# Operand sums of the second half moved one slot forward, score products moved two slots back, in a fused attention and gated-FFN kernel

## The chip, the cores and the metric

The kernel runs on one core of a Trainium2 chip. The metric is the time of one execution on the device in microseconds (us). The kernel before takes 808.18 us, the median of three runs (807.96 to 809.92). The execution that was profiled took 805.96 us and its span from the first to the last instruction is 804.2 us.

## The reference, cut to what matters

```python
# q, k, v: (4, 6016, 256); w_gate, w_val: (256, 1536); w_out: (1536, 256)
qn = q / (norm(q, axis=1) + 1e-6);  kn = k / (norm(k, axis=1) + 1e-6)   # norm over the 6016 tokens
s  = kn.T @ qn / tau                       # (4, 256, 256), contracted over tokens
a  = softmax(s)                            # over the last axis
x  = (v @ a).reshape(24064, 256)
out = (sigmoid(x @ w_gate) * (x @ w_val)) @ w_out      # (24064, 256)
```

So there are four batches. Each needs a 256x256 score matrix and two vectors of norms before its tokens can pass through the gated FFN.

## The kernel before, in words

**Folding.** The kernel never forms `x`. It multiplies the softmax weights of a batch into `w_gate` and `w_val` once (the tiles `gh_G` and `gh_H`) and feeds the transposed `v` straight into these.

**Tiles and slots.** A batch has 47 tiles of 128 tokens, in 12 chunks of four tiles (512 tokens), the last of three. A chunk has 12 *slots*, one for each 128 of the 1536 hidden columns. The loop at the end of the kernel runs over batches `b`, chunks `ci` and slots `f`; the order of instructions on every engine is the order in which this loop writes them (a manual schedule), and the engines run against each other only through semaphores.

**A slot.** `glu` (L660) issues two matmuls into `ps_gate`, a tanh of it on the scalar engine (ACT) into `g_sb` (L680), two matmuls into `ps_val`, and one operation on the vector engine (DVE), which writes 128 rows of the hidden tile `hT` (L683). `ps_gate` and `ps_val` have two buffers each. Between the two pairs of matmuls, `run_work` issues a share of the output product of the *previous* chunk, one part in (12 - f) of what is left.

**The output product.** `out_work` (L720) multiplies `hT` of the previous chunk by `w_out` with seven products in place of eight per 2x2 block, which is Winograd's form of Strassen's scheme. Its operands are sums of blocks of `hT`, five kinds, m = 0 to 4, made by `a_sum` (L694) on DVE into the tile `sums` (L705). A chunk's sums are made in two halves: g = 0 from hidden rows 0 to 5 of the chunk's slots, g = 1 from rows 6 to 11. The first half is made in slots 7 to 11 of the chunk itself (`OWN_SLOTS`), the second while the next chunk runs (`NEXT_SLOTS`), since its `hT` is complete only then. In the order of `ORDER`, each product runs i = 0 to 5; from i = 3 on it reads the second half. For a chunk of four tiles that is 84 products, seven in a slot. The product `z1` (sum m = 1) of the first pair of tiles reaches i = 3 as the first product of slot 3, `x2` (m = 3) in slot 5, `y2` (m = 2) in slot 6, `z2` (m = 0) in slot 7 and `v2` (m = 4) in slot 8. For a chunk of three tiles `z1` reaches i = 3 in slot 2. `sums` of g = 1 has one buffer.

**The next batch's scores.** While batch b is in its FFN, `side_work` (L931) places the work for batch n = b + 1 in the slots, after `glu` and the operand sums of the slot. For b = 1 and 2 the token tiles come in six groups of eight (the last of seven), a group for every 16 slots from s0 on. `score_sums` (L340) makes operand sums of q and k, again five kinds, into the tiles `qs`: m = 0 in slot s0, 2 in s0 + 3, 3 in s0 + 6, 4 in s0 + 9 on DVE (L351, L359, L364), and m = 1 by two DMA transfers. `queue_scores` (L922) puts the group's 28 matmuls into a queue, and `run_scores` (L925) takes an even share of them in each slot, from s0 + 3 to s0 + 18. The products that read m = 4 begin with number 12 of the 28, which comes in slot s0 + 11. After the last group come folds of the squares (`acc_fold`, L312, line L315, DVE) in slots 95, 96, 98 and 100 of the batch, and `score_out` copies the scores away in slots 103 and 105.

Of the kernel before, what the change touches and what calls it, by code (L numbers as in the profile page):

```python
# [45 lines left out]
    (0, "x2"), (0, "y2"), (0, "z2"), (0, "v2"),  # L46
    (1, "x2"), (1, "y2"), (1, "z2"), (1, "v2"),
)
NEXT_SLOTS = {1: 1, 3: 3, 4: 2, 5: 0, 6: 4}
OWN_SLOTS = {7: 1, 8: 3, 9: 2, 10: 0, 11: 4}  # L50


# [1 line left out]
def kernel(  # L54
# [109 lines left out]
    t0, nt = groups0[0]  # L164
# [529 lines left out]
    def a_sum(b, ci, g, m):  # L694

        nt = groups[ci][1]
        half = nt // 2
        hT = hts[b, ci]
        if (b, ci, g) not in sums:
            sums[b, ci, g] = spool.tile(  # L700
                [P, len(A_SUMS), FC // 4, CH // 2], BF16, tag=f"s{g}", name="sums", bufs=2 - g
            )
        (r0, k0), op, (r1, k1) = A_SUMS[m]
        f0, f1 = g * (FC // 2), (g + 1) * (FC // 2)
        nc.vector.tensor_tensor(  # L705
            out=sums[b, ci, g][:, m, :, : half * P],
            in0=hT[:, f0 + k0 : f1 : 2, ds(r0 * half * P, half * P)],
            in1=hT[:, f0 + k1 : f1 : 2, ds(r1 * half * P, half * P)],
            op=op,
        )  # L710
# [94 lines left out]
    def run_work(work, share):  # L805

        upto = sum(w[0] for w in work) * share
        done = 0
        while work and done < upto:
            cost, fn, *args = work.pop(0)  # L810
            fn(*args)
            done += cost

    def store():
        while stores:
            b, ci = stores.pop(0)
            t0, nt = groups[ci]
            nc.sync.dma_start(out=out_rows[b][:, t0 : t0 + nt, :], in_=ffn.pop((b, ci))[:, :nt, :])
# [112 lines left out]
    def side_work(b):  # L931


        side = {}

        def at(slot, fn, *a):
            side.setdefault(divmod(slot, FC), []).append((fn, a))

        for ci in range(NCH):
            nb, nci = (b, ci + 1) if ci + 1 < NCH else (b + 1, 0)  # L940
            lb, lci = (b, ci + 2) if ci + 2 < NCH else (b + 1, ci + 2 - NCH)
            if nb < B:
                at(ci * FC + 2, transpose_v, nb, nci)
            if lb < B:
                at(ci * FC + (10 if (b, ci) == (0, 0) else 0), load_v, lb, lci)
            if (b, ci) == (0, 0):
                for i in range(FC // TPC):
                    at(8, copy_w_out, i)
                for n, m in enumerate((1, 0, 3, 2, 4)):
                    for i in range(FC // TPC):  # L950
                        at(11 + 2 * n, sum_w_out, m, i)
        n = b + 1
        if n == B:
            return side
        first, last = (14 if b == 0 else 0), 8 * FC
        wide = [(t, min(2 * TPC, NT - t)) for t in range(0, NT, 2 * TPC)]
        at(first, acc_start, n)
        for g, (t0, nt) in enumerate(groups if b == 0 else []):
            s0 = first + g * (last - first) // NCH
            at(max(FC - 3, s0 - 12), load_qk, n, t0, nt)  # L960
            for u in range(nt):
                at(first + (t0 + u) * (last - first) // NT, score, n, t0, u)
            for w in range(2):
                at(s0 + 1 + 4 * w, narrow_square, n, g, w)
                slot = s0 + 3 + 4 * w
                at(slot + 2 if w == 0 and slot % FC == 8 else slot, narrow_add, n, g, w)
        step = (last - first) / len(wide)
        for g, (t0, nt) in enumerate(wide if b else []):
            s0 = first + int(g * step)
            halves = [(0, nt - TPC), (TPC, TPC)]  # L970
            if s0 >= 24:
                at(s0 - 24, load_qk, n, t0, nt)
            for i in range(4):
                at(s0 + 3 * i, acc_square, n, t0, 1 - i // 2, halves, i % 2)
            for w in range(2):
                at(s0 + 11 - 6 * w, acc_add, n, t0, w, halves)
            for m in (0, 2, 3, 4):
                at(s0 + 3 * max(0, m - 1), score_sums, n, t0, m, halves)
            ahead = 0 if g == 0 else 5
            at(s0 + 1 - ahead, score_sums, n, t0, 1, halves)  # L980
            at(s0 + 6 - ahead, score_sum_q, n, t0, halves)
            end = first + int((g + 1) * step) + 3
            at(s0 + 3, queue_scores, n, t0, halves)
            for slot in range(s0 + 3, end):
                at(slot, run_scores, s0 + 3, end, slot)
        if n + 1 < B:
            for g, (t0, nt) in enumerate(wide[:2]):
                at(NCH * FC - 24 + 16 * g, load_qk, n + 1, t0, nt)
        s0 = 8 * FC + 2
        if b == 0:  # L990
            at(s0, acc_fold, n, 0, (2, 1))
            at(s0 + 1, acc_fold, n, 1, (2, 1))
            at(s0 + 3, norms_mm, n)
            at(s0 + 4, root_seed, n)
            at(s0 + 4, root_steps, n)
            at(s0 + 10, norms_inv, n)
            at(s0 + 11, spread_both, n)
            at(s0 + 13, read_row, n)
        else:
            at(s0 - 3, acc_fold, n, 1, (4,))  # L1000
            at(s0 - 2, acc_fold, n, 1, (2, 1))
            at(s0, acc_fold, n, 0, (4,))
            at(s0 + 2, acc_fold, n, 0, (2, 1))
            at(s0 + 5, score_out, n, 0)
            at(s0 + 6, norms_mm, n)
            at(s0 + 7, score_out, n, 1)
            at(s0 + 7, root_seed, n)
            at(s0 + 7, root_steps, n)
            at(s0 + 12, norms_inv, n)
            at(s0 + 12, spread_both, n)  # L1010
            at(s0 + 14, read_row, n)
            at(s0 + 14, score_blocks, n)
        at(s0 + 22, scale_x, n, 0)
        at(s0 + 24, scale_x, n, 1)
        at(s0 + 25, exps, n, 0)
        at(s0 + 26, exps, n, 1)
        at(s0 + 28, all_sums, n)
        at(s0 + 28, gh_tiles, n)
        for i, piece in enumerate(gh_order):
            slot = s0 + 29 + 2 * i  # L1020
            if slot < NCH * FC:
                at(slot, gh, n, piece, *((pss, "s"), (psm, "m"))[i % 2])
            else:
                spill.setdefault((n, *divmod(slot - NCH * FC, FC)), []).append((gh, (n, piece, psm, "m")))
        return side
# [7 lines left out]
    def gh_pieces(ns):  # L1033
        for n in ns:
            gh(0, gh_first[n], *gh_banks[n % 4])

    prev = None
    for b in range(B):
        side = side_work(b)
        for ci in range(NCH):  # L1040
            final = (b, ci) == (B - 1, NCH - 1)
            for f in range(FC):
                mid = gh_mid.get(f) if (b, ci) == (0, 0) else None
                if prev is not None:
                    mid = lambda: run_work(work, 1 / max(1, FC - final - f))
                elif mid is not None:
                    mid = lambda ns=mid: gh_pieces(ns)
                glu(b, ci, f, mid)
                if prev is not None:
                    if f == 4:  # L1050
                        store()
                    if f + final in NEXT_SLOTS and prev != (0, 0):
                        a_sum(*prev, 1, NEXT_SLOTS[f + final])
                if f in OWN_SLOTS and not final and (b, ci) != (0, 0):
                    a_sum(b, ci, 0, OWN_SLOTS[f])
                for fn, a in spill.get((b, ci, f), []) + side.get((ci, f), []):
                    fn(*a)
                if (b, ci) == (0, 0):
                    gh_pieces(gh_end.get(f, ()))
            prev = (b, ci)  # L1060
            if not final:
                work = out_work(*prev)
# [39 lines left out]
```

## Time and profile before

The page gives each engine's busy time over the span of 804.2 us.

| Engine | busy us | share | instructions |
|---|---|---|---|
| TensorE, matmul (PE) | 781.5 | 97% | 6861 |
| TensorE, weight load (PEld) | 497.0 | 62% | 6875 |
| VectorE (DVE) | 705.0 | 88% | 1228 |
| ScalarE (ACT) | 513.8 | 64% | 891 |
| GpSimd (POOL) | 396.8 | 49% | 618 |

The groups that the change touches, or that stand next to it on their engine:

| Line | work | count | mean ns |
|---|---|---|---|
| L683 | `hT` from `g_sb` and `ps_val`, DVE | 576 | 672 |
| L705 | `sums`, DVE | 460 | 582 |
| L364 | `qs`, m = 3 and 4, DVE | 28 | 682 (median) |
| L129 | matmul into `ps_gate` or `ps_val` | 1152 each | 375 |
| L129 | matmul into `ps_o` that reads `sums` | 2670 | 219 |

The duration of a matmul is its latency. Matmuls overlap, so 375 ns isn't the time that one adds to the stream. In the same way one DVE operation begins some 0.07 us before the record of the one in front of it ends. For both, the distance from start to start is what counts. In every view, "A <- B" means that A waited and B is what it waited for.

### The profile page before, as it was taken

To read this page: it belongs to the slowest core of one execution; us is meant where nothing else is said; L and a number is where in the kernel's file an instruction comes from. 1 tells how busy PE (TensorE), PEld (TensorE's weight loads), DVE (VectorE), ACT (ScalarE), POOL (GpSimd) and SP (SyncE) were. 2 spreads that over 40 slices of the span, in tenths; PEclk is the share of its full clock that TensorE was granted. 3 is DMA by queue.
4 is the path that set the end of the run, shared out by engine and by line. 5 is a ranking of instruction groups with operands and counts; after the bars stand their busy time and mean duration, and the time that the engine had idled before them with its cause. 6 is when DMAs were issued, how large, how long until landed. Compare 5 with 4: busy or idle time off the path is not lost.

```text
span 804.2 us, 18203 instructions
## 1 busy us (share of the span) xinstructions
PE 781.5 (97%) x6861; PEld 497.0 (62%) x6875; DVE 705.0 (88%) x1228; ACT 513.8 (64%) x891; POOL 396.8 (49%) x618
## 2 busy tenths in 40 slices
PE   3899999999999999999999999999999999999998
PEld 2556666666666666665665666666666566666666
DVE  5768999999889889999988899999998888888886
ACT  3766777765666767665667666766666555555554
POOL 3564444436443466564833555664653234434433
PEclk9999999999999999999999999999999999999999
DMA  9997757422776999962577599866243323433302
GB/s 212 205 194 131 131 102 141 88 60 54 143 143 129 171 179 165 192 116 53 108 138 149 126 165 203 178 136 128 51 71 81 63 62 75 79 59 73 80 27 73
DMA packets 82776, 95.16 MB, mean 118 GB/s; under 512 B 52512, under 2 KB 58528, under 8 KB 82688
## 3 DMA queue, kind: packets, MB, share of 16 engines
q0 software_dynamic: 25616, 55.85, 38.9%
q1 hardware_dynamic: 56496, 37.30, 20.9%
q8 instruction: 53, 0.87, 0.4%
q10 hardware_dynamic: 576, 0.85, 0.4%
q14 instruction: 35, 0.29, 0.1%
HBM read 79.04 MB, written 24.64 MB: 129 GB/s over the span
## 4 chain that ended last, share of the span: by engine, by line
PE 89%; DVE 5%; DMA 4%; issue 1%; ACT 0%; POOL 0%; DVEq 0%; ACTq 0%; POOLq 0%
PE ps_val L129 29%; PE ps_gate L129 28%; PE ps_o L129 26%; DMA qk_sb<-in_k_dram 4%; PE ps_s L129 3%; PE ps_gh L129 2%; DVE hT L683 2%; DVE sums L705 1%; DVE acc L315 1%; DVE qs L364 0%; PE ps_end L129 0%; ACT m_sb L759 0%; ACT g_sb L680 0%; DVE x_sb L543 0%; PE ps_n L129 0%
## 5 line engine op out<-in xcount | busy, mean ns | idle before, releaser
L680 ACT ACTIVATE g_sb<-ps_gate 128x512 f32<-128x512 f32 (+1 forms) x576 | 338.5, 588 | 255.7 <-PE ps_gate L129 248.7
L683 DVE SCALAR_TENSOR_TENSOR hT<-g_sb,ps_val 128x512 bf16<-128x512 f32 (+1 forms) x576 | 386.5, 672 | 80.1 <-PE ps_val L129 50.9
L129 PE MATMUL ps_gate<-vT,gh_G 128*128 128x512 bf16 (+1 forms) x1152 | 337.6, 375 | 0.1
L129 PE MATMUL ps_val<-vT,gh_H 128*128 128x512 bf16 (+1 forms) x1152 | 337.5, 375 | 0.0
L705 DVE TENSOR_TENSOR sums<-hT 128x768 bf16<-128x768 bf16 (+1 forms) x460 | 267.7, 582 | 0.0
L129 PEld LDWEIGHTS <-sums 128*128 128x128 bf16 x2670 | 182.0, 98 | 88.3 <-DVE sums L705 8.9
L776 POOL TENSOR_TENSOR out_sb<-out_sb,m_sb 128x256 f32<-128x256 f32 x89 | 69.4, 780 | 184.0 <-ACT out_sb L766 159.5
L129 PE MATMUL ps_o<-w_sums,sums 128*128 128x128 bf16 x1602 | 156.1, 219 | 2.4 <-DVE sums L705 2.1
L129 PEld LDWEIGHTS <-gh_G 128*128 128x128 bf16 x1152 | 104.2, 98 | 82.2 <-DVE gh_G L629 0.3
L129 PEld LDWEIGHTS <-hT 128*128 128x128 bf16 x1200 | 88.3, 98 | 46.8
L760 POOL TENSOR_TENSOR m_sb<-m_sb 128x128 f32<-128x128 f32 x89 | 43.5, 489 | 136.3 <-ACT m_sb L759 136.2
L129 PE MATMUL ps_o<-w_out_sb,sums 128*128 128x128 bf16 x1068 | 96.6, 219 | 0.1
L129 PE MATMUL ps_o<-w_sums,hT 128*128 128x128 bf16 x1068 | 95.5, 219 | 0.0
L129 PEld LDWEIGHTS <-gh_H 128*128 128x128 bf16 x1152 | 90.1, 98 | 3.3 <-DVE gh_H L629 0.3
L777 POOL TENSOR_TENSOR out_sb<-out_sb 128x256 f32<-128x256 f32 x89 | 80.7, 907 | 7.0
L761 POOL TENSOR_TENSOR m_sb<-m_sb 128x128 f32<-128x128 f32 x89 | 61.6, 692 | 7.0
L129 PEld LDWEIGHTS <-qk_sb 128*128 128x128 bf16 x286 | 29.5, 103 | 43.4 <-issue 9.9
L766 ACT COPY out_sb<-ps_o 128x512 f32<-128x512 f32 x89 | 51.7, 581 | 0.1
L129 PE MATMUL ps_s<-qk_sb 128*128 128x256 bf16 (+1 forms) x194 | 34.7, 297 | 15.5 <-DMA qk_sb<-in_k_dram 8.5
L257 ACT ACTIVATE sq<-qk_sb 128x1024 bf16<-128x1024 bf16 (+3 forms) x36 | 35.7, 1011 | 12.0 <-DMA qk_sb<-in_k_dram 11.9
L759 ACT COPY m_sb<-ps_o 128x384 f32<-128x384 f32 x89 | 42.1, 474 | 1.1 <-PE ps_o L129 1.0
L297 ACT ACTIVATE sq<-qk_sb 128x1024 bf16<-128x1024 bf16 (+1 forms) x40 | 41.4, 1035 | 0.0
(102 smaller groups left out, 450.3 us busy)
## 6 DMA issues: line engine op xcount, KB each, us to landing
out_dram<-out_sb SPq DMA_DIRECT2D x43, 512.0 KB, 3.4
v_sb<-in_v_dram POOLq DMA_DIRECT2D x44, 256.0 KB, 5.4
acc<-sq POOLq DMA_DIRECT2D x16, 512.0 KB, 6.7
qk_sb<-in_q_dram POOLq DMA_DIRECT2D x14, 512.0 KB, 10.3
qk_sb<-in_k_dram POOLq DMA_DIRECT2D x14, 512.0 KB, 8.3
qs<-qk_sb POOLq DMA_DIRECT2D x20, 256.0 KB, 5.0
qk_sb<-in_q_dram POOLq DMA_DIRECT2D x15, 256.0 KB, 4.5
qk_sb<-in_k_dram POOLq DMA_DIRECT2D x15, 256.0 KB, 5.9
```

The lines of the kernel that those rows point to most:

```text
L129: nc.tensor.matmul(out, lhsT=lhsT, rhs=rhs, start=start, stop=stop, **kw)
L257: nc.scalar.activation(out=sq[:, :nt, :], in_=src[:, :nt, :], func=ACT.Square)
L297: nc.scalar.activation(out=s["sq", w][:, u0 : u0 + n, :], in_=src[:, u0 : u0 + n, :], func=ACT.Square)
L680: nc.scalar.activation(out=g_sb[:, :n], in_=ps_gate[:, :n], func=ACT.Tanh, scale=0.5)
L683: nc.vector.scalar_tensor_tensor(out=hts[b, ci][:, f, :n], in0=g_sb[:, :n], scalar=1.0, in1=ps_val[:, :n], op0=ALU.add, op1=ALU.mult,)
L705: nc.vector.tensor_tensor(out=sums[b, ci, g][:, m, :, : half * P], in0=hT[:, f0 + k0 : f1 : 2, ds(r0 * half * P, half * P)], in1=hT[:, f0 ...
L759: nc.scalar.copy(m, states[p]["ps"][:, : 3 * P].rearrange("p (n c) -> p n c", c=P))
L760: nc.gpsimd.tensor_tensor(out=m[:, 1, :], in0=m[:, 1, :], in1=m[:, 2, :], op=ALU.add)
L761: nc.gpsimd.tensor_tensor(out=m[:, 2, :], in0=m[:, 1, :], in1=m[:, 0, :], op=ALU.add)
L766: nc.scalar.copy(o[:, p : p + half + 1 : half, :], states[p]["ps"].rearrange("p (t c) -> p t c", c=C),)
L776: add(out=ends, in0=ends, in1=states[p]["m"][:, 1:3, :], op=ALU.add)
L777: add(out=ends, in0=ends, in1=mids, op=ALU.subtract)
```

## The change

It has two parts, both of order alone. No instruction is added or removed.

- `NEXT_SLOTS` gets keys that are one lower. The second half's sums are made in slots 0, 2, 3, 4, 5 of the next chunk, not in 1, 3, 4, 5, 6. It is for TensorE: a sum is to be ready earlier ahead of the product that reads it. In the last chunk of all, where the output product runs through faster, the old code already made them a slot sooner (`f + final`); there the slots stay what they were.
- Each group's score products begin in slot s0 + 5 and end in s0 + 20, two later than before, so that the sums `qs` have two more slots to be made in.

```diff
-NEXT_SLOTS = {1: 1, 3: 3, 4: 2, 5: 0, 6: 4}
+NEXT_SLOTS = {0: 1, 2: 3, 3: 2, 4: 0, 5: 4}
...
-            end = first + int((g + 1) * step) + 3
-            at(s0 + 3, queue_scores, n, t0, halves)
-            for slot in range(s0 + 3, end):
-                at(slot, run_scores, s0 + 3, end, slot)
+            end = first + int((g + 1) * step) + 5
+            at(s0 + 5, queue_scores, n, t0, halves)
+            for slot in range(s0 + 5, end):
+                at(slot, run_scores, s0 + 5, end, slot)
...
-                    if f + final in NEXT_SLOTS and prev != (0, 0):
-                        a_sum(*prev, 1, NEXT_SLOTS[f + final])
+                    if f in NEXT_SLOTS and prev != (0, 0):
+                        a_sum(*prev, 1, NEXT_SLOTS[f])
```

## Prediction

> **What bounds the kernel now.** I read the page first: busy times and the chain that ended last.
>
> ```profile
> PE 781.5 (97%) x6861; PEld 497.0 (62%) x6875; DVE 705.0 (88%) x1228; ACT 513.8 (64%) x891; POOL 396.8 (49%) x618
> ...
> PE 89%; DVE 5%; DMA 4%; issue 1%; ACT 0%; POOL 0%; DVEq 0%; ACTq 0%; POOLq 0%
> ```
>
> TensorE ends the chain for 89% of the span, and the 4% of DMA are the first loads. DVE's 5% are the only part in the body that is not the stream of matmuls. The change adds and removes no work, so all it can win is the time in which that stream stands still. The view of waits names the candidates (total us, times, longest):
>
> ```profile
> PEld L129 <- DVE sums L705: 8.9, 21, 0.9
> ...
> PE ps_o L129 <- DVE sums L705: 2.1, 7, 0.4
> ...
> PE ps_s L129 <- DVE qs L364: 0.2, 1, 0.2
> ```
>
> These bracket the loss and don't give it: weight loads run ahead, so 8.9 is more than the stream loses, while a modelled matmul end covers part of a gap, so 2.1 is less. Hence I took distances from start to start out of the timeline. Two pieces of the chain at the kernel's end give the undisturbed pace:
>
> ```profile
> 797.39 2.62 PE ps_o L129 x24
> 800.01 1.36 PE ps_end L129 x24
> ```
>
> 24 matmuls of 256 columns in 2.62 us are 0.109 each; 24 of 128 columns take 0.057 with the latency of the last, 0.053 inside a run; two of 512 columns take 0.43. A chunk's slot without scores is thus 2 x 0.43 + 7 x 0.053 = 1.23 us, and the timeline of the last batch shows 1.25. Where two starts lie further apart, the rest is lost. The worst stretch is chunk 8 of batches 1 and 2:
>
> ```profile
> 365.45 0.59 PE L129 MATMUL ps_gate<-vT,gh_G 128*128 128x512 bf16 x2
> 365.81 0.55 DVE L705 TENSOR_TENSOR sums<-hT 128x768 bf16<-128x768 bf16 x1
> ...
> 366.42 0.34 PE L129 MATMUL ps_o<-w_sums,sums 128*128 128x128 bf16 x3 [0.37 <-DVE sums L705]
> ```
>
> The two gate matmuls of slot 3 begin at 365.45 and need 0.43, so `z1` could begin at 365.88; it begins at 366.42, 0.06 after the sum of slot 1 ends: 0.54 lost, of which the brackets show 0.37. Going through the timeline for every gap over 0.07 us after the first 45 us, and leaving out gaps of one matmul's length at `ps_gh` (there a record is missing), I find 20, each ending some 0.06 after a sum on DVE:
> - 18 end with a second-half sum: in batch 0, 0.09, 0.12, 0.27; in slot 1 of the three chunks behind a three-tile chunk, 0.43, 0.60, 0.25; with m = 4 in slot 6 of an ordinary chunk, 0.32, 0.48, 0.11; five of 0.08 to 0.14 in chunks 3 and 7, together 0.55; in chunk 8 of batches 1 and 2, 0.54 + 0.36 and 0.55 + 0.35. Sum 5.0.
> - 2 end with the m = 4 sum of a score group: 0.36 and 0.11. Sum 0.47.
>
> Together about **5.4 us**, 0.67% of the time. Everything else in these 20 stretches is TensorE at its own pace.
>
> **What the Trainium skill says.** "Perfetto Trace Analysis", Identifying the Most-Contended Engine, calls matmul busy time a bad measure of headroom. The trace agrees: of the 0.54 above, busy time hides 0.17, so I counted starts. "TensorE: Matmul & The Clock Gate", Architectural detail, says that TensorE pulls weight loads ahead of matmuls while DVE is a strict queue. Both show: PEld's wait exceeds the loss, and a sum on DVE waits for whatever was issued in front of it. "Perfetto Trace Analysis", Optimizing Scalar/DVE Operations, says that the second half of a DVE instruction's latency overlaps the next. Here a sum that lasts 0.54 is followed after 0.47 (371.31 to 371.78), and `hT` of 0.67 after 0.60. I use these two.
>
> **The change part by part.**
>
> *The second-half sums, 230 of the 460.* Four of five go one slot forward, past one `hT`, and m = 1 goes in front of `hT` of slot 1. The gain is the distance to the `hT` in front: at least 0.60 us where DVE is back to back, 1.25 where it waits for TensorE. The largest gap is 0.60, and in most gaps the sum also escapes a `qs`, fold or `ps_gh` operation that was in front of it or in its slot. So the 18 gaps close as far as the sums cause them. Buffers add no wait: the g = 1 tile's last reader is in slot 11 of the chunk before, which TensorE has passed before `hT` of slot 0 can begin.
>
> What queues behind a sum on DVE is the next `hT`, and behind that the `ps_val` pair two slots on, which reuses its bank. The prefix count shows who pays: by `hT` of slots 1 and 3 to 6 DVE has made one sum more than before, by slots 2 and 7 the same number. So each of these can be late by at most 0.47 more. I compared the end of every `hT` with the start of the `ps_val` pair two slots later: the smallest room, from chunk 1 on, is 0.92 at slot 1 and 0.70 to 0.81 at slots 3 to 6. All exceed 0.47, so nothing new stalls by that alone. But a closed gap also brings TensorE forward. In chunk 8 DVE has no rest to give:
>
> ```profile
> 361.50:373.50 12.00, 11.44 (x105) 7.05 (x103) 11.92 (x21) 6.53 (x13) 4.01 (x7) 1.00 0.41 89
> 664.00:676.00 12.00, 12.00 (x105) 7.33 (x103) 10.23 (x19) 7.30 (x14) 4.63 (x7) 1.00 0.57 89
> ```
>
> The columns after the mean are PE, PEld, DVE, ACT, POOL: DVE 11.92 of 12.00 in chunk 8, against 10.23 in the last batch. At `hT` of slot 5 the room is 0.81; less 0.47, less the 0.90 by which TensorE now comes sooner, it is -0.56. The later score products put 4 x 0.053 = 0.21 of matmuls into slots 99 and 100 of the batch, which are slots 3 and 4 of this chunk, and TensorE comes that much later: -0.35. So I take 0.35 of a new wait in each of the two chunks, 0.7 in all. Elsewhere the worst is slot 4 of chunk 0: 0.70 - 0.60 = 0.10 left, where DVE was idle just before (the wait there is for ACT), so the 0.47 doesn't carry over.
>
> *The score products two slots later.* 28 matmuls a group, none added. The room between m = 4 and its first reader grows from two slots to four, some 2.6 us more against 0.36: **0.47 won**. Each `qs` is read by s0 + 20 at the latest (m = 1, two buffers, rewritten from s0 + 28), m = 0 by s0 + 10 and rewritten at s0 + 16: no wait. The last group ends in slot 100, ahead of the copy in 103. Cost zero, since TensorE does the same matmuls in other slots.
>
> *The last chunk's slots* stay, so nothing moves there.
>
> Sum: 5.4 - 0.7 = 4.7 gained. 808.2 - 4.7 = **803.5 us**.
>
> **The rivals.**
> - *The gaps close* as above: 803.5. For it: each gap ends with one sum, and DVE catches up within a few slots (10.23 of 12.00 busy in the last batch). 70%.
> - *DVE gives half back.* A sum can grow to 1.18 us (309.38) where GpSimd is at work; "SBUF — State Buffer", SBUF: two separate sides, says that one of the two fully blocks while the other holds their shared ports. If such stretches let the `hT` pay in chunks 3, 7, 8 and in batch 0, only the 1.29 behind three-tile chunks, the 0.91 of m = 4, the 0.47 of scores and a little remain, some 2.8: 805.4. 14%.
> - *The wait only moves* from the sum to `ps_val`, everywhere DVE is late: 808.2. Against it: in slots without gaps the room at `ps_val` is 1.1 to 1.3. 9%.
> - *Slower.* Slot 0 is where DVE is latest: `hT` of slot 0 starts over 0.9 behind its matmuls in eight chunks. If the m = 1 sum overflows the room there (0.47 each, 8 x 0.47 = 3.8) and nothing is won: 812. Against it: slot 1's room of 0.92 and no sum in slot 1 after. 7%.
>
> **How the numbers follow.** Faster by over 0.3% means below 805.8: the first case and most of the second, 0.80. Within 0.3%: 0.13. Slower: 0.07. The largest gain is the whole 5.4 and some gaps below 0.07, near 6, less the runs' own scatter: low end 801.9. The upper end takes in the half case with a margin: 806.4. That leaves out the last two cases, 16%, and a little of the others.
>
> **What would show it.** In the profile after: the waits for `sums` L705 on PEld and PE nearly gone; no wait of `ps_s` for `qs`; DVE's busy time still near 705; a small new wait of `ps_val` for `hT` L683 around 370 and 564; chunk 0 of batches 1 to 3 shorter by 0.25 to 0.6 each. The prediction is wrong if waits for L683 add up to what L705 loses, if the sums themselves get longer because they now meet GpSimd's work, or if the gaps for L705 persist although made a slot sooner.

## The result, and the profile after

The changed kernel takes **803.28 us** (median of six runs, 802.42 to 804.45) against 808.07 us (806.87 to 809.92) for the kernel before in the same comparison. The ratio is 0.9941 with a 95% interval of 0.9926 to 0.9956: faster by 4.8 us, between 3.6 and 6.0. The forecast was 803.5.

The page of the changed kernel, engines' busy time and the chain that ended last:

```profile
PE 779.1 (97%) x6861; PEld 498.0 (62%) x6875; DVE 706.9 (88%) x1228; ACT 513.1 (64%) x891; POOL 395.5 (49%) x618
...
PE 92%; DMA 4%; DVE 3%; issue 1%; ACT 0%; POOL 0%; DVEq 0%; POOLq 0%
```

The counts of instructions are the same as before, and DVE is as busy (706.9 us against 705.0). DVE's part of the chain has gone from 5% to 3%, and TensorE's from 89% to 92%. So the same work lies nearer to TensorE's own pace. Who waited for the sums is told by the answer for the tile `sums`, L705:

```profile
who waited for it (us, times):
  ACT g_sb L680: 0.7, 1
```

Neither TensorE nor its weight loads wait for a sum any more; before, these were 2.1 us in 7 waits and 8.9 us in 21. A line that the first trace of the kernel before did not have stands in the view of waits:

```profile
PE ps_val L129 <- DVE hT L683: 1.9, 3, 1.2
```

This is the wait that the prediction placed in chunk 8, and something more: the longest of the three, 1.2 us, is elsewhere. Counted from start to start, as in the prediction, the gaps over 0.07 us after the first 45 us are these. All 20 of before (5.4 us) are closed. New ones are `ps_val` behind `hT` in chunk 8 of batches 1 and 2 (0.15 and 0.48 us in each), 0.28 at the norm matmuls of batch 0, 0.13 at a score matmul of batch 0 (behind a load, L148; waits of 0.12 to 0.28 there come and go in traces with and without the change), and 1.41 in slot 2 of chunk 3 of batch 2.

This count can be tested against the whole. From the gate matmuls of slot 6 of the first chunk (46.15 us before, 46.05 after) to the start of the last matmul, TensorE takes 754.98 us before and 752.03 after. Less the gaps, that is 749.5 and 749.0, and the other traces of these two kernels taken below give the same two numbers. So almost nothing is left out: the 0.5 us between them are gaps under 0.07 us, which close as well.

In chunk 8 it looks like this (TensorE's timeline, then DVE's):

```profile
368.78 0.59 PE L129 MATMUL ps_gate<-vT,gh_G 128*128 128x512 bf16 x2
369.22 0.55 PE L129 MATMUL ps_o<-w_sums,sums 128*128 128x128 bf16 x7
370.09 0.59 PE L129 MATMUL ps_val<-vT,gh_H 128*128 128x512 bf16 x2 [0.32 <-DVE hT L683]
```
```profile
367.83 0.54 DVE L705 TENSOR_TENSOR sums<-hT 128x768 bf16<-128x768 bf16 x1
368.30 1.14 DVE L315 TENSOR_TENSOR acc<-acc 128x512 bf16<-128x512 bf16 x2
369.36 0.67 DVE L683 SCALAR_TENSOR_TENSOR hT<-g_sb,ps_val 128x512 bf16<-128x512 f32 x1
```

Seven products from 369.22 need 0.39 us, so the `ps_val` pair of slot 7 could begin at 369.61. It begins at 370.09, when `hT` of slot 5 has freed the bank. In front of that `hT` stand the sum of slot 4 and a pair of folds. This pair lasted 0.94 us in the kernel before and lasts 1.14 here, and the fold ahead of `hT` of slot 3 has grown too (before, then after):

```profile
366.88 0.68 DVE L315 TENSOR_TENSOR acc<-acc 128x1024 bf16<-128x1024 bf16 x1
367.52 0.69 DVE L683 SCALAR_TENSOR_TENSOR hT<-g_sb,ps_val 128x512 bf16<-128x512 f32 x1
```
```profile
365.30 0.94 DVE L315 TENSOR_TENSOR acc<-acc 128x1024 bf16<-128x1024 bf16 x1
366.17 0.67 DVE L683 SCALAR_TENSOR_TENSOR hT<-g_sb,ps_val 128x512 bf16<-128x512 f32 x1
```

### The profile page after: what moved, and what is told of

Read it like the earlier page. It is cut to its first block, busy times and chain, and to the rows that moved or that the text cites. A ratio compares the mean times of both kernels' runs of the same rounds, so it can differ in the third digit from the quotient of the medians.

```text
span 801.1 us, 18203 instructions
## 1 busy us (share of the span) xinstructions
PE 779.1 (97%) x6861; PEld 498.0 (62%) x6875; DVE 706.9 (88%) x1228; ACT 513.1 (64%) x891; POOL 395.5 (49%) x618
## 4 chain that ended last, share of the span: by engine, by line
PE 92%; DMA 4%; DVE 3%; issue 1%; ACT 0%; POOL 0%; DVEq 0%; POOLq 0%
PE ps_val L129 30%; PE ps_gate L129 29%; PE ps_o L129 27%; DMA qk_sb<-in_k_dram 4%; PE ps_s L129 4%; PE ps_gh L129 2%; DVE hT L683 1%; DVE acc L315 1%; DVE sums L705 1%; PE ps_end L129 0%; DVE qs L359 0%; PE ps_n L129 0%; DVE x_sb L543 0%; PE ps_r L129 0%; ACT e_sb L561 0%
## 5 line engine op out<-in xcount | busy, mean ns | idle before, releaser
L705 DVE TENSOR_TENSOR sums<-hT 128x768 bf16<-128x768 bf16 (+1 forms) x460 | 273.7, 595 | 0.0
L129 PE MATMUL ps_o<-w_sums,sums 128*128 128x128 bf16 x1602 | 154.2, 219 | 0.0
L760 POOL TENSOR_TENSOR m_sb<-m_sb 128x128 f32<-128x128 f32 x89 | 44.5, 499 | 138.9 <-ACT m_sb L759 138.7
L761 POOL TENSOR_TENSOR m_sb<-m_sb 128x128 f32<-128x128 f32 x89 | 58.5, 658 | 7.0
```

The source lines that it names most:

```text
L129: nc.tensor.matmul(out, lhsT=lhsT, rhs=rhs, start=start, stop=stop, **kw)
L705: nc.vector.tensor_tensor(out=sums[b, ci, g][:, m, :, : half * P], in0=hT[:, f0 + k0 : f1 : 2, ds(r0 * half * P, half * P)], in1=hT[:, f0 ...
L760: nc.gpsimd.tensor_tensor(out=m[:, 1, :], in0=m[:, 1, :], in1=m[:, 2, :], op=ALU.add)
L761: nc.gpsimd.tensor_tensor(out=m[:, 2, :], in0=m[:, 1, :], in1=m[:, 0, :], op=ALU.add)
```

## The experiments

Each time and ratio is set against the kernel before on the same chip. Only the order of instructions differs between all these kernels.

**Each part alone.** `sums_only` keeps the new `NEXT_SLOTS` and takes the score products back:

```diff
-            end = first + int((g + 1) * step) + 5
-            at(s0 + 5, queue_scores, n, t0, halves)
-            for slot in range(s0 + 5, end):
-                at(slot, run_scores, s0 + 5, end, slot)
+            end = first + int((g + 1) * step) + 3
+            at(s0 + 3, queue_scores, n, t0, halves)
+            for slot in range(s0 + 3, end):
+                at(slot, run_scores, s0 + 3, end, slot)
```

> The sums one slot sooner, score products left where the kernel before has them. Theory (lead of the sums): the 18 gaps behind second-half sums close, 5.0 us; chunk 8 of batches 1 and 2 waits anew for hT, 0.63 each as in the changed kernel plus up to 0.21 each, since the score products no longer fill slots 3 and 4 there, about 1.7 together; the two gaps for qs of 0.36 and 0.11 stay. Gain about 3.3: 804.8 us. Rival (the later score products carry the gain): within 0.5 us of before, 808.

Measured: 805.42 us, ratio 0.9962 (0.995 to 0.9974), 3.1 us faster. All gaps behind sums are closed. The gap of slot 7 of chunk 8 is 0.77 us in both batches, against 0.48 with both parts:

```profile
370.02 0.55 PE L129 MATMUL ps_o<-w_sums,sums 128*128 128x128 bf16 x7
371.18 0.38 PE L129 MATMUL ps_val<-vT,gh_H 128*128 128x512 bf16 x1 [0.61 <-DVE hT L683]
```

(370.02 + 0.39 = 370.41; begun at 371.18.) So the four score matmuls that the second part brings into slots 3 and 4 of this chunk are worth 0.29 there, where the prediction took 0.21. The two gaps for `qs` were expected to stay, and neither is left in this trace. So their 0.47 can't be put down to the second part; what they go with is told below, at `before_sumq`.

`scores_only` has the second part alone, with the old `NEXT_SLOTS`:

```diff
-NEXT_SLOTS = {0: 1, 2: 3, 3: 2, 4: 0, 5: 4}
+NEXT_SLOTS = {1: 1, 3: 3, 4: 2, 5: 0, 6: 4}
...
-                    if f in NEXT_SLOTS and prev != (0, 0):
-                        a_sum(*prev, 1, NEXT_SLOTS[f])
+                    if f + final in NEXT_SLOTS and prev != (0, 0):
+                        a_sum(*prev, 1, NEXT_SLOTS[f + final])
```

> Score products from slot 5 of their group, sums left where the kernel before has them. Theory: the two qs gaps close (0.47 us), and 4 matmuls more in slots 3 and 4 of chunk 8 let its slot-7 gap shrink by 0.21 in batches 1 and 2 (0.42): about 0.9 gained, 807.2 us, not told from no change by the times; the 18 gaps behind sums stay but for that. Rival (score products carry the gain): 4 to 5 us gained, 803.5.

Measured: 808.26 us, ratio 0.9998 (0.999 to 1.0006). The score products don't carry the gain. My 0.9 was too much: the `qs` gaps are gone, but the slot-7 gap in chunk 8 stays at 0.35 in both batches. In the old order `hT` of slots 3 and 4 waits for TensorE (it begins 0.11 us after the recorded end of its matmuls), so four more matmuls delay both alike.

**One sum of five.** `m1_only` is the kernel before with m = 1 in slot 0:

```diff
-NEXT_SLOTS = {1: 1, 3: 3, 4: 2, 5: 0, 6: 4}
+NEXT_SLOTS = {0: 1, 3: 3, 4: 2, 5: 0, 6: 4}
+FINAL_SLOTS = {0: 1, 2: 3, 3: 2, 4: 0, 5: 4}
...
-                    if f + final in NEXT_SLOTS and prev != (0, 0):
-                        a_sum(*prev, 1, NEXT_SLOTS[f + final])
+                    slots = FINAL_SLOTS if final else NEXT_SLOTS
+                    if f in slots and prev != (0, 0):
+                        a_sum(*prev, 1, slots[f])
```

> Of the kernel before, only the m = 1 sum of the second half goes from slot 1 to slot 0; the other four and the score products stay. Theory: gaps at z1 close: 1.28 us behind the three-tile chunks and 0.27 in chunks 3 and 7; in chunk 8 the 0.54 and 0.55 close too, but DVE has no rest there, so the slot-1 hT costs 0.15 and the slot-7 gap grows from 0.36 to about 0.75 in both batches: nothing won there. The m = 4 gaps stay. Gain about 1.5: 806.6 us. Rival (m = 1 carries all the gain, the other four moves are idle): 803.5.

Measured: 806.86 us, ratio 0.9987 (0.9978 to 0.9995), 1.1 us faster. The gaps at `z1` are gone. In chunk 8 a wait of 0.15 for `hT` of slot 1 comes in, m = 2 now costs 0.13, and the slot-7 gap has grown from 0.35 to 0.81: 1.09 us a batch against 0.89 before. In this chunk nothing is won by hurrying one sum. (This trace is of the slowest of its 13 runs, 809.02 us, and has some 4.6 us of the waits by chance that are looked at below.)

**The direction turned round.** `late4` puts m = 3, 2, 0, 4 of the kernel before one slot later:

```diff
-NEXT_SLOTS = {1: 1, 3: 3, 4: 2, 5: 0, 6: 4}
+NEXT_SLOTS = {1: 1, 4: 3, 5: 2, 6: 0, 7: 4}
```

with the last chunk's slots as they were, as in `m1_only`.

> The kernel before with the four sums m = 3, 2, 0, 4 one slot later (slots 4, 5, 6, 7), m = 1 and the last chunk as they were: the change's direction turned round. Theory (lead against the first reader is what counts): such a sum ends 1.2 us after its slot's ps_val pair, and its first reader stands 0.43 of gate matmuls and 1 to 4 products into the slot after, so TensorE stands still some 0.6 us four times in each of 42 chunks: about 100 us slower, 910. Rival (DVE's total work sets the time and the slots hardly matter): within 5 us of before, 808.

Measured: 946.41 us (one run). Its waits (the lines lie one further down):

```profile
PEld L130 <- DVE sums L706: 154.6, 178, 1.2
PE ps_o L130 <- DVE sums L706: 115.9, 172, 1.0
```

There are 42 gaps at each of the four sums, of 0.80 us (m = 3, 2), 0.90 (m = 0) and 0.89 (m = 4) in the mean: 42 x 3.39 = 142 us, and the span grew by 944.6 - 804.2 = 140. The lead of a sum over its first reader is what counts. The size was missed (0.85, not 0.6) mostly because I counted from the recorded end of a pair of matmuls, 0.59 us after its start, while the stream moves on after 0.43, which is 0.16 sooner.

**The changed kernel again.** A second trace shows what belongs to the order and what doesn't.

> The changed kernel once more, unedited, for a second trace. Theory: the waits of ps_val for hT in chunk 8 of batches 1 and 2 (0.15 and 0.48 each) and the 0.28 at the norm matmuls of batch 0 come back to within 0.05, since they follow from the order; the 1.40 us at chunk 3 of batch 2 is chance (a sum of 1.87 us beside GpSimd's out_sb adds) and comes back with another size, at another place or not at all. Rival: it belongs to the order and comes back at 1.4. Time 803.3 either way.

Measured: 804.72 us, ratio 0.9951 (0.9938 to 0.9965). The chunk-8 waits came back at 0.15 and 0.49 (0.48) in both batches, the norm matmuls at 0.28. The 1.41 did not come back in this size: chunk 3 of batch 2 showed 0.56, chunk 3 of batch 1 0.86 and slot 1 of chunk 6 of batch 1 1.30, where the first trace had nothing. A second trace of the kernel before was taken for the same purpose:

> The kernel before once more, for a second trace. Theory: the 18 gaps behind sums come back to within 0.1 each where no long DVE operation is near; besides, one to four waits of ps_val for hT or longer gaps of 0.5 us and more by chance, near L369, as the traces with its sums in the old slots had them. Rival: none, as in the first trace.

Measured: 809.27 us (one run). The gaps behind sums add up to 4.8 us (5.0 before), and besides there are waits of `ps_val` for `hT` of 1.39, 0.54 and 0.32. The first trace of before, on which the prediction rests, was of a run of 805.96 us, 2.1 below the median, and had none of these.

"By chance" needs a limit. Seven traces with the transfer of L369 in its old slot show such waits, and in all of them every wait of `ps_val` for `hT` of 0.5 us and more, apart from those in chunk 8, lies in one of four places: slot 2 of chunk 3 or slot 1 of chunk 6, in batch 1 or 2. Each follows an issue of L369 within four slots. So where they can come follows from the order; whether a wait comes there, and how long it is, changes from run to run.

**What the waits by chance are.** GpSimd's timeline in the changed kernel, ahead of the 1.41, and the DVE operations that it met:

```profile
471.71 0.88 POOL L369 DMA_DIRECT2D qs<-qk_sb  x1 [3.01 <-DMA qs<-qk_sb]
472.33 1.02 POOL L776 TENSOR_TENSOR out_sb<-out_sb,m_sb 128x256 f32<-128x256 f32 x1
473.43 0.93 POOL L777 TENSOR_TENSOR out_sb<-out_sb 128x256 f32<-128x256 f32 x1
```
```profile
471.91 1.87 DVE L705 TENSOR_TENSOR sums<-hT 128x768 bf16<-128x768 bf16 x1
473.70 1.21 DVE L359 TENSOR_TENSOR qs<-qk_sb 128x1024 bf16<-128x1024 bf16 x1
```

L369, the accumulating transfer of the m = 1 score sum, stands in GpSimd's queue until the transfer of L355 has landed, and the `out_sb` adds stand behind it. When they run at last, a sum of 0.55 us lasts 1.87 beside them and the next operation 1.21 instead of 0.68. In this trace the 159 sums of 128x768 that ran beside nothing on GpSimd took 0.54 to 0.55 us, the two beside L369 alone 0.54 and 0.55, the 76 beside both `out_sb` adds without L369 0.54 to 1.02, and the three beside L369 and both adds 1.33, 1.43 and 1.87. So it is the adds right behind L369 that go with the longest sums, not the transfer's issue by itself. `sumq_late` issues L369 four slots later:

```diff
-            at(s0 + 6 - ahead, score_sum_q, n, t0, halves)
+            at(s0 + 10 - ahead, score_sum_q, n, t0, halves)
```

> The changed kernel with the accumulating transfer of the m = 1 score sum (L369) issued four slots later, nothing else. Theory (L369 stands in GpSimd's queue until the first transfer has landed; the out_sb adds pile up behind it and then block a DVE operation): the wait of L369 falls from 25 us to under 5, no sums or qs operation beside L369 and L776 above 1.3 us, and single waits of ps_val for hT of 0.7 us and more outside chunk 8 are gone: about 1 us better than the changed kernel, 802.3. Rival (GpSimd's queue doesn't matter): 803.3, long operations stay.

Measured: 801.95 us, ratio 0.9924 (0.9911 to 0.9937). The wait of L369 in the changed kernel, and the same line with the edit:

```profile
POOL qs L369 <- DMA qs<-qk_sb: 25.3, 7, 4.8
```
```profile
POOL qs L369 <- DMA qs<-qk_sb: 2.4, 1, 2.4
```

No DVE operation lasts more than 1.22 us, and outside chunk 8 no wait of `ps_val` for `hT` exceeds 0.08. The same edit was made to the kernel before, and the changed one with it was repeated beside it:

> The kernel before with L369 four slots later, nothing else. Theory (the waits of 0.5 to 1.4 us by chance come from GpSimd's queue behind L369 and burden the kernel before as well, though its first trace had none of them): the trace keeps the gaps behind sums (5.0 us, within 0.5) and the waits by chance go; the time is that of the changed kernel with the same edit plus the gaps that the change closes less those it makes, 802.0 + 5.4 - 1.5 = 805.9 us. Rival (chance burdens the changed kernel alone): 808.2, as before.

> The changed kernel with L369 four slots later, once more, to stand on the same chip beside the kernel before with the same edit: 802.0 us, 3.9 below it. If the change won its 4.8 in part by making chance waits rarer, the distance here is smaller than 4.8; if not, it is 4.8.

Measured: 806.08 us, ratio 0.9981 (0.9969 to 0.9992), and 802.60, ratio 0.9934 (0.9921 to 0.9946). The kernel before gains 2.0 us too, so chance burdens both. Their traces, nearly free of it, have 5.04 us of gaps behind sums and none. With everything over 0.07 counted, it is 5.67 against 1.73 us: 3.9 apart, and 4.4 with the 0.5 of smaller gaps. The medians are 3.5 apart.

The trace of `before_sumq` has no gap for `qs` either, though it holds no part of the change; both traces of the kernel before with L369 in its old slot have them. Ahead of the second gap the two L364 operations last 1.68 and 1.21 us in the first trace of before and 0.69 each here. So moving L369 alone closes these two gaps as well, and `m1_only`, whose score products stay where they were, has none either: nothing shows that it was the later score products.

**The folds in chunk 8.** `folds_moved` spreads them without adding work (in batch 0, not shown, the first fold goes one slot forward and the norm matmuls one slot back):

```diff
-            at(s0 - 3, acc_fold, n, 1, (4,))
-            at(s0 - 2, acc_fold, n, 1, (2, 1))
-            at(s0, acc_fold, n, 0, (4,))
-            at(s0 + 2, acc_fold, n, 0, (2, 1))
+            at(s0 - 6, acc_fold, n, 1, (4,))
+            at(s0 - 4, acc_fold, n, 1, (2, 1))
+            at(s0 - 1, acc_fold, n, 0, (4,))
+            at(s0 + 4, acc_fold, n, 0, (2, 1))
```

> The changed kernel with the folds of the squares spread out: slots 92, 94, 97 and 102 of the batch in place of 95, 96, 98 and 100 (batches 1 and 2), slot 97 for 98 and the norm matmuls one slot later in batch 0. No work added or removed. Theory (the new waits in chunk 8 are DVE work bunched in slots 11 and 0 to 4): the waits of ps_val for hT at slots 3 and 7 of chunk 8 (0.63 a batch, twice) and the 0.28 at the norm matmuls of batch 0 go: about 1.5 gained against the changed kernel, 801.8 us. Rival (DVE's total in that stretch is the bound, wherever the folds are): the waits move to other slots, 803.3.

Measured: 803.95 us, ratio 0.9956 (0.9943 to 0.9969): nothing won over the changed kernel. The waits in chunk 8 and at the norm matmuls of batch 0 are gone, but in both batches the `ps_val` pair of slot 1 of chunk 8 has a new one of 0.80, for the `hT` of slot 11 of chunk 7. (The trace also has 3.4 us of waits by chance.) TensorE, then DVE ahead of it, then GpSimd:

```profile
362.00 0.55 PE L129 MATMUL ps_o<-w_sums,hT 128*128 128x128 bf16 x7
363.19 0.59 PE L129 MATMUL ps_val<-vT,gh_H 128*128 128x512 bf16 x2 [0.63 <-DVE hT L683]
```
```profile
357.59 1.21 DVE L315 TENSOR_TENSOR acc<-acc 128x1024 bf16<-128x1024 bf16 x1
...
360.86 1.68 DVE L315 TENSOR_TENSOR acc<-acc 128x512 bf16<-128x512 bf16 x2
```
```profile
360.62 0.90 POOL L776 TENSOR_TENSOR out_sb<-out_sb,m_sb 128x256 f32<-128x256 f32 x1 [2.36 <-ACT out_sb L766]
361.60 0.79 POOL L777 TENSOR_TENSOR out_sb<-out_sb 128x256 f32<-128x256 f32 x1
```

The last two folds of w = 1 together last 1.68, against 0.74 in the kernel before (364.56), where no operation of GpSimd ran beside them. A wait moved, as the rival said; whether the total is the bound needed another place. `best` takes slots 97, 99, 102 and 103, away from slots 8 to 11 of a chunk, with L369 late as well (the removed fold lines are those shown above):

```diff
-            at(s0 + 6 - ahead, score_sum_q, n, t0, halves)
+            at(s0 + 10 - ahead, score_sum_q, n, t0, halves)
...
+            at(s0 - 1, acc_fold, n, 1, (4,))
+            at(s0 + 1, acc_fold, n, 1, (2, 1))
+            at(s0 + 4, acc_fold, n, 0, (4,))
+            at(s0 + 5, acc_fold, n, 0, (2, 1))
...
+            at(s0 + 7, norms_mm, n)
```

and the rest of the norms chain one slot later; in batch 0 the first fold goes a slot forward and the norm matmuls a slot back.

> The changed kernel with L369 four slots later and the folds spread over slots 97, 99, 102 and 103 of the batch (the first and third have no sum after the change; none meets slots 8 to 11, where GpSimd's adds run), the norms chain one slot later to match; in batch 0 slot 97 for 98 and norm matmuls one slot later. Theory: the chunk-8 waits (1.26 together) and the 0.28 go as well: 800.8 us. Rival (DVE's total in chunk 8 is the bound): as sumq_late, 802.3, with the waits at other slots of chunks 7 to 9.

Measured: **800.85 us** (800.8 to 801.45), ratio 0.9909 (0.9895 to 0.9923), 7.3 us under the kernel before. No wait of `ps_val` for `hT` above 0.08 is left. In the gaps over 0.07 us it has 0.8 in all, against 2.0 for `sumq_late`; the norm matmuls wait 0.32 for the last fold in batches 1 and 2:

```profile
371.51 0.59 PE L129 MATMUL ps_val<-vT,gh_H 128*128 128x512 bf16 x2
372.26 0.25 PE L129 MATMUL ps_s<-ones_bf,acc 128*128 128x1 bf16 x4 [0.15 <-DVE acc L315]
```

All four folds now lie inside chunk 8 and its waits for `hT` are gone. So the place of the folds set the wait in chunk 8, not DVE's total.

## Why the prediction was right

The likeliest case came true: 803.28 against 803.5, faster. Its steps, one by one:

- **The gaps behind sums (5.0) and `qs` (0.47) close.** All 20 are gone, and no sum is waited for by TensorE; but the two for `qs` are gone with L369 alone moved, too. `sums_only`, `m1_only` and `late4` show that the lead is the cause of the 18, the last in the other direction.
- **No new wait elsewhere.** Right for the slots, but the 0.28 at the norm matmuls of batch 0 was missed: I looked at `hT` and the bank of `ps_val` alone, while the fold of slot 3 also stands behind a sum, and the norm matmuls wait for it.
- **A new wait of 0.35 in chunk 8, twice.** The mechanism was right, the size too small: 0.63, twice. Slot 1 was left out. I compared its room of 0.93 with 0.47 alone; but the closed gap of 0.54 lies ahead of the `ps_val` pair of slot 3, which needs that bank, so the room is 0.93 - 0.47 - 0.54 = -0.08, and 0.15 was measured. The term for slot 5 (0.81 - 0.47 - 0.90 + 0.21 = -0.35) measured 0.48, and here the delay of `hT` was too small. Counted from the first `ps_val` pair of the chunk, `hT` of slot 5 ended at 9.21 us before and at 9.91 after: 0.70 later, not 0.47. The prediction let every other operation last as before, but the fold and the pair of folds shown above now run beside both of GpSimd's `m_sb` adds, before beside one of them. From start to start they take 0.87 and 1.06 in place of 0.64 and 0.86, while one sum there takes 0.47 in place of 0.65. TensorE in turn comes 0.90 - 0.21 - 0.15 = 0.54 sooner, since 0.15 is lost at slot 3 already. So the room is 0.81 - 0.70 - 0.54 = -0.43, and TensorE begins 0.06 after `hT` ends: 0.49, against 0.48 measured. The folds have the new lengths in all four traces of the changed kernel and the old ones in all three of the kernel before, with L369 early or late. The sum of new waits is thus 1.5 and not 0.7.
- **The sum, 4.7.** By gaps it should have been 5.4 - 1.5 = 3.9 and, with the 0.5 of gaps under 0.07 us that were not in the sum, 4.4. The intervals of the two comparisons of these kernels (3.6 to 6.0 and 2.8 to 5.0) contain both; with the chance waits taken out of both, the medians are 3.5 apart, each known to about 1 us. So part of the agreement to 0.2 us is luck: a term that was too small and one that was left out work against each other, and the first trace of before happened to be free of chance waits.
- **The score products cost nothing and win 0.47.** They cost nothing, and alone they can't be told from no change. But the 0.47 can't be credited to them, and what the traces show the second part to add to the first is the shorter wait in chunk 8, 0.29 twice. The times (3.1 us faster without it, 4.0 and 4.8 with it) have overlapping intervals and don't settle more.
- **Rivals.** "DVE gives half back" named the right thing, sums that grow beside GpSimd, but it strikes the kernel before as well. One of the signs that I had named for a wrong prediction, sums that get longer, did show in small: their mean went from 582 and 586 ns in two traces of before to 595 and 591 in two of the changed kernel, and with L369 late from 579 to 587 and 588. TensorE waits for none of them. "The wait only moves" holds for chunk 8 and for about 1.5 of 5.4 us. "Slower", a sum in slot 0 that overflows the room there, shows only as the 0.15 in chunk 8, twice.
- **The overlap on DVE.** The prediction speaks of the second half of an operation's latency. In the traces an operation overlaps the next one by 0.06 to 0.07 us (0.54 followed after 0.47, 0.67 after 0.60), not by half of its length. The sums above use the measured distances, so nothing in them changes.

Whether the change makes the chance waits rarer stays open: two traces of before had 0 and 2.2 us of them, two of the changed kernel 1.4 and 2.7.

## What to carry to other kernels

When one engine sets the pace, count its loss from start to start and find for each gap the one instruction that ends it; a producer placed one slot sooner then wins what the gaps add up to, less what its new place delays. To find the latter, test the room of *every* buffer that frees later against both the delay and the time by which the closed gaps bring the leading engine forward, and ask of each operation in the way whether it will now run beside another engine's work and last longer. And an instruction that waits for a transfer at the head of a queue harms through what piles up behind it, so issue it when the transfer has landed.

## What the runs showed of the hardware that I had not expected

- A bf16 addition of 128x768 on DVE takes 0.55 us alone. In the traces of the kernel before and the changed one it took up to 1.18 beside two GpSimd additions of 0.9 to 1.0 us each, and up to 1.87 where these ran right behind the issue of L369; beside that issue alone it stayed at 0.55. A longer queue on GpSimd thus becomes lost time on TensorE two engines further on, though GpSimd is busy for half of the span.
- The scatter of single runs has more than one source. The waits behind L369 are one (0 to 2.7 us in the traces of these two kernels). The start is another: the gate matmuls of slot 6 of the first chunk begin between 45.9 and 47.5 us in eight traces: two each of the kernel before and the changed one, the three with L369 late alone, and `best`. In one comparison nine runs of the kernel before spread over 2.6 us (807.56 to 810.13), five of the changed kernel over 2.1 (803.23 to 805.36), five with L369 late over 1.9 (801.54 to 803.43), and five of `best` over 0.65 (800.8 to 801.45). Which part of `best` narrows it isn't shown.
